# A recurrent attention step whose streamed weights are spread over the step and whose ring slots are released one by one

## The chip, the cores and the metric

The kernel runs on one core of one Trainium2 chip. The metric is device time in microseconds (us), the median over several executions. TensorE (PE) multiplies, and its weight loads (PEld) overlap its matmuls; ScalarE (ACT), VectorE (DVE) and GpSimd (POOL) do the rest, and SyncE (SP) does nothing here but issue DMA transfers.

## The reference

Two branches over 2048 rows of width 1024 are mixed by a gate. Branch A is a recurrence over 64 segments of 32 rows: each step attends over 8 memory rows and 32 new rows (40 columns) with 32 heads of 128, and the first 8 rows of its result are the next step's memory. Branch B is a feed-forward layer of width 3584.

```python
for s in range(n_seg):                      # 64
    h = concatenate([mem, x[:, s*32:(s+1)*32]], axis=1)      # 40 rows
    q, k, v = (einsum('btd,dhe->bhte', h, W) for W in (Wq, Wk, Wv))
    p = softmax(where(mask, q @ k.T * scale, -1e9))
    o = einsum('bhte,hed->btd', p @ v, Wo)
    mem = o[:, :8]; outs.append(o[:, 8:])
b = (gelu(x @ w_gate) * (x @ w_up)) @ w_down
return g * a + (1 - g) * b                  # g = sigmoid((x * gate_w).sum(-1))
```

## The kernel before

There are two blocks, one after the other: the recurrent chain (lines up to 693) and the feed-forward part (lines 695 to 999). Only the chain is touched. Within each block every engine has an instruction list in the order in which the Python code emits it; engines meet only at semaphores, which are written out by hand.

**Weights.** Wq, Wo and the K weights of heads 0 to 15 (`kres`) stay in SBUF. The K weights of heads 16 to 31 and all V weights are streamed anew in each step: a *slab* is the weights of four heads, 1 MB, and a step needs twelve, eight of V and four of K. They go into `ring`, which has three slots. `emit_slab` (L268) puts one transfer on SP's queue (L277), and it waits until the slab three before it has been used.

**A step.** The projections are cut into *blocks*: one matrix and one head, eight accumulating matmuls with their weight loads (L603), 40 columns of a PSUM bank. Blocks are grouped into *chunks*, which alternate between two PSUM banks, and ScalarE copies a finished chunk to `qkvT` (L623, L625 for K and Q, L630 for V). With four groups of eight heads the order of chunks is: K and Q of group 0 (six heads, then two), V of group 0; the same for group 1; K and Q of groups 2 and 3; V of group 2; V of group 3. That is twelve chunks. Attention work is hung between chunks by `add_hook`: scores (`emit_scores`, L392) with the softmax on VectorE and ScalarE (L403 to L422), the transposes of V (`emit_vtr`, L444), of the probabilities (`emit_pt`, L466), and the product with V (`emit_pv`, L492). Scores follow the group's last K/Q chunk at once, V's transposes follow the V chunk at once, the probabilities' transposes come two chunks after the scores. After the last chunk come what is left of attention, the transposes of the next rows of x (L512), and 256 matmuls with Wo (L663); ScalarE copies their result to `a_evac` and, as memory, to the next step's `hT` (L677), for which the next step's first chunk waits. The result of a step is transposed (`emit_atr`, L536) after the next step's first chunk.

**How slots come free.** Only the last block of a chunk raises a semaphore, and a slab is free when its chunk is done:

```python
E("pe", mk, waits=bw, inc=(S_QKV_DONE, 1) if last else None)
if streamed and h % 4 == 3:
    slab_free_target[slab_index(mat, h)] = C + 1
    emit_slab(slab_emit_count[0])
```

A V chunk uses two slabs, so both slots come free at its end.

Of the kernel before, what the change touches and what calls it, by code (L numbers as in the profile page):

```python
# [7 lines left out]
ACTF = mybir.ActivationFunctionType  # L8
# [79 lines left out]
def bass_gated_mix__memory_aug_recurrent_mem_tr__geglu_ffn__prompt_kernel(  # L88
# [47 lines left out]
    with ExitStack() as es_top:  # L136
        cnt = [0]

        def new_sem(name):
            cnt[0] += 1  # L140
            h = es_top.enter_context(nc.semaphore(f"{name}_{cnt[0]}"))
            return _Sem(h)
# [3 lines left out]
        with ExitStack() as es:  # L146
# [43 lines left out]
            S_SLOT = [new_sem(f"slot{i}") for i in range(RING)]  # L190
            S_QKV_DONE = new_sem("qkvdone")
            S_QKV_EVAC = new_sem("qkvevac")
            S_PINIT = new_sem("pinit")
            S_XTR_DONE = new_sem("xtrdone")
            S_HT = new_sem("htready")
# [34 lines left out]
            E("pool", lambda e: e.dma_start(stage[32:64, :], xf[0:SEG, :]), inc=(S_XLOAD, 16))  # L230
            E("pool", lambda e: e.dma_start(stage[64:64 + M, :], mem0[:, :]), inc=(S_XLOAD, 16))

            chunk_list = []
            if NG_ATT >= 2:
                for gq in range(NG_ATT - 2):
                    chunk_list += [("kqa", gq), ("kqb", gq), ("v", gq)]
                gA, gB = NG_ATT - 2, NG_ATT - 1
                chunk_list += [("kqa", gA), ("kqb", gA), ("kqa", gB), ("kqb", gB), ("v", gA), ("v", gB)]
            else:
                chunk_list += [("kqa", 0), ("kqb", 0), ("v", 0)]  # L240
            NCH = len(chunk_list)

            def chunk_blocks(kind, gq):
                hs = list(range(gq * 8, gq * 8 + 8))
                if kind == "kqa":
                    return [(m, h) for h in hs[0:6] for m in ("k", "q")]
                if kind == "kqb":
                    return [(m, h) for h in hs[6:8] for m in ("k", "q")]
                return [("v", h) for h in hs]
# [5 lines left out]
            for kind, gq in chunk_list:  # L255
                for mat, h in chunk_blocks(kind, gq):
# [111 lines left out]
            for s in range(NSEG):  # L368
# [8 lines left out]
                def emit_scores(gq):  # L377
                    gg = att_base + gq
                    b = gg % 2
                    slot = gq % 2  # L380
                    waits = [(S_QKV_EVAC, kqb_evac_target[gq])]
# [146 lines left out]
                def emit_atr(sp):  # L528
# [12 lines left out]
                    if sp >= 1:  # L541
# [3 lines left out]
                    E("pool", lambda e, sp=sp: e.dma_start(a_scr[sp * SEG:(sp + 1) * SEG, :], stage[0:SEG, :]),  # L545
                      waits=[(S_ASTG, sp + 1)], inc=(S_ASTORE, 16))

                if s == 0:
                    xtr_last_evac_box = [xtr_last_evac]
                pos = {ck: i for i, ck in enumerate(chunk_list)}  # L550
                hooks = {}
                END = NCH

                def add_hook(k, fn):
                    k = min(k, END)
                    hooks.setdefault(k, []).append(fn)

                kqb_evac_target = {}
                v_evac_target = {}
                hook_pri = {}  # L560
                for gq in range(NG_ATT):
                    k_sc = pos[("kqb", gq)] + 1
                    k_vt = pos[("v", gq)] + 1
                    k_pt = k_sc + 2
                    k_pv = max(k_pt, k_vt) + 1
                    for k, pri, fn in ((k_sc, 1, lambda gq=gq: emit_scores(gq)), (k_vt, 0, lambda gq=gq: emit_vtr(gq)),
                                       (k_pt, 3, lambda gq=gq: emit_pt(gq)), (k_pv, 2, lambda gq=gq: emit_pv(gq))):
                        add_hook(k, fn)
                        hook_pri[fn] = (min(k, END), k, pri, gq)
                if s >= 1:  # L570
                    fn_atr = lambda: emit_atr(s - 1)
                    add_hook(1, fn_atr)
                    hook_pri[fn_atr] = (1, 1, -1, 0)

                for ci, (kind, gq) in enumerate(chunk_list):
                    C = chunk_base + ci
                    bank = C % 2
                    blocks = chunk_blocks(kind, gq)
# [8 lines left out]
                    for bi, (mat, h) in enumerate(blocks):  # L587
                        bw = list(cw) if bi == 0 else []
                        if s == 0:
                            if mat == "q":  # L590
                                bw.append((S_WQ[h // 4], 16))
                            if mat == "k" and h < KRES_H:
                                bw.append((S_KRES[h // 4], 16))
                        streamed = is_streamed(mat, h)
                        if streamed and h % 4 == 0:
                            i = slab_index(mat, h)
                            bw.append((S_SLOT[i % RING], 16 * (i // RING + 1)))
                        lhs_list = [lhsT_for(mat, h, kc) for kc in range(KC)]

                        def mk(e, lhs_list=lhs_list, bank=bank, bi=bi, cur=cur):  # L600
# [11 lines left out]
                    view = PB[bank][:, 0:len(blocks) * L]  # L612
                    aw = [(S_QKV_DONE, C + 1)]
                    gg = att_base + gq
                    if kind == "kqa" and gg - 2 >= 0:
                        aw.append((S_SC_DONE, gg - 2 + 1))
                    if kind == "v" and gg - 2 >= 0:
                        aw.append((S_VTR_DONE, gg - 2 + 1))
                    if kind in ("kqa", "kqb"):
                        nh = 6 if kind == "kqa" else 2  # L620
                        h0 = 0 if kind == "kqa" else 6
                        v3 = view.rearrange("p (hh m c) -> p m hh c", m=2, c=L)
                        E("act", lambda e, v3=v3, slot=slot, h0=h0, nh=nh: e.activation(  # L623
                            qkvT[:, slot, h0:h0 + nh, :], v3[:, 0, :, :], ACTF.Copy), waits=aw)
                        E("act", lambda e, v3=v3, slot=slot, h0=h0, nh=nh: e.activation(  # L625
                            qkvT[:, slot, 8 + h0:8 + h0 + nh, :], v3[:, 1, :, :], ACTF.Copy), inc=(S_QKV_EVAC, 1))
                        if kind == "kqb":
                            kqb_evac_target[gq] = C + 1
                    else:
                        E("act", lambda e, view=view, slot=slot: e.activation(  # L630
                            qkvT[:, slot, 16:24, :], view.rearrange("p (hh c) -> p hh c", c=L), ACTF.Copy),
                          waits=aw, inc=(S_QKV_EVAC, 1))
                        v_evac_target[gq] = C + 1
                    assert S_QKV_EVAC.n == C + 1
                    for fn in hooks.get(ci + 1, []) if (ci + 1) < END else []:
                        fn()
# [396 lines left out]
```

## Time and profile before

| | |
|---|---|
| median of 5 runs | 4465.7 us (4456.75 to 4469.58) |
| profiled execution, its own time | 4458.04 us |
| span of the profiled execution | 4456.3 us |
| TensorE matmul busy, share of the span | 73% |
| TensorE weight loads busy | 65% |
| VectorE, ScalarE, GpSimd busy | 25%, 21%, 2% |
| mean granted TensorE clock | 0.748 |
| DMA, mean over the span | 221 GB/s |

The span runs from the first to the last instruction. Engines overlap, so shares do not add up. The granted clock is a share of 2.4 GHz; 0.50 is the lower level, 1.2 GHz. "issue" is a wait for nothing that the profile shows. Matmuls are pipelined and the end of one is modelled, so starts are the better measure of pace.

### The profile page before, as it was taken

What the parts mean: (1) busy time and instruction counts of PE and PEld (TensorE: products, weight loads), DVE (VectorE), ACT (ScalarE), POOL (GpSimd) and SP (SyncE); (2) the same over time, 40 slices, a digit from 0 to 9 for tenths busy, and PEclk for the clock granted to TensorE, in tenths of its full rate; (3) what the DMA queues carried; (4) which work ended last, traced back from release to release, by engine and by line L of the source; (5) the groups of instructions that cost most, each with busy time, mean ns of one, the idle gap of its engine ahead of it and who ended that gap; (6) DMA issues with size and microseconds to landing.
All of it is one profiled execution on the core that took longest, in us unless ns stands there. A gap on an engine that the chain in (4) does not pass through costs nothing. (4 is left out here: it accounts for less than half of the span.)

```text
span 4456.3 us, 169380 instructions
## 1 busy us (share of the span) xinstructions
PE 3266.0 (73%) x79440; PEld 2899.5 (65%) x79512; DVE 1122.7 (25%) x2577; ACT 947.2 (21%) x2818; POOL 82.0 (2%) x165
## 2 busy tenths in 40 slices
PE   3677777777777677777767677677777766699998
PEld 3666666666666666666666666666666666577776
DVE  1222222212222222222212222222222212355555
ACT  1122221222222222212212222222222111122222
POOL 0000000000000000000000000000000000000000
PEclk7777676767667777776767676777777766799999
DMA  9677676767777676766767777676767666766665
GB/s 327 209 223 226 216 224 213 226 218 222 226 230 231 215 220 208 224 213 213 230 212 231 230 231 230 212 221 213 226 211 233 215 213 200 233 209 204 214 207 166
DMA packets 945191, 982.96 MB, mean 221 GB/s; under 512 B 17256, under 2 KB 930664, under 8 KB 944496
## 3 DMA queue, kind: packets, MB, share of 16 engines
q1 hardware_dynamic: 937904, 955.31, 67.8%
q0 software_dynamic: 6592, 16.81, 1.2%
q8 instruction: 628, 10.29, 1.0%
q14 instruction: 67, 0.55, 0.0%
HBM read 963.66 MB, written 8.39 MB: 218 GB/s over the span
## 5 line engine op out<-in xcount | busy, mean ns | idle before, releaser
L603 PE MATMUL pb<-hT,ring 128*128 128x40 bf16 x24576 | 992.7, 194 | 680.9 <-DMA ring<-in_A_Wv_dram 385.9
L603 PEld LDWEIGHTS pb<-hT,ring 128*128 128x128 bf16 x24576 | 848.8, 106 | 760.6 <-DMA ring<-in_A_Wv_dram 314.6
L603 PE MATMUL pb<-hT,wq 128*128 128x40 bf16 x16384 | 798.6, 189 | 56.7 <-issue 53.6
L603 PEld LDWEIGHTS pb<-hT,wq 128*128 128x128 bf16 x16384 | 618.9, 102 | 51.5 <-issue 48.4
L663 PE MATMUL pb<-oT,wo 128*128 128x40 bf16 x16384 | 513.3, 193 | 90.4 <-issue 76.6
L663 PEld LDWEIGHTS pb<-oT,wo 128*128 128x128 bf16 x16384 | 500.2, 105 | 103.1 <-issue 82.7
L623 ACT ACTIVATE qkvT<-pb 128x240 bf16<-128x240 f32 (+1 forms) x512 | 155.4, 304 | 1180.8 <-PE pb L603 1180.8
L403 DVE SCALAR_TENSOR_TENSOR sm<-pb,mask 40x320 f32<-40x320 f32 x256 | 123.5, 482 | 1115.1 <-PE pb L392 1115.1
L603 PE MATMUL pb<-hT,kres 128*128 128x40 bf16 x8192 | 372.4, 181 | 19.6 <-ACT hT L677 18.2
L451 DVE COPY vsb<-pb 40x1024 bf16<-40x1024 bf16 x256 | 174.1, 680 | 763.7 <-PE pb L444 763.5
L444 PE MATMUL pb<-ident,qkvT 128*40 128x128 bf16 x2048 | 230.6, 280 | 144.7 <-ACT qkvT L630 134.3
L603 PEld LDWEIGHTS pb<-hT,kres 128*128 128x128 bf16 x8192 | 280.9, 96 | 42.3 <-ACT hT L677 25.2
L444 PEld LDWEIGHTS pb<-ident,qkvT 128*40 128x40 bf16 x2048 | 171.1, 130 | 174.9 <-ACT qkvT L630 164.3
L543 DVE COPY stage<-pb 32x1024 bf16<-32x1024 bf16 x64 | 43.4, 679 | 911.8 <-PE pb L536 911.8
L630 ACT ACTIVATE qkvT<-pb 128x320 bf16<-128x320 f32 x256 | 111.9, 437 | 737.6 <-PE pb L603 737.3
L892 PE MATMUL psh<-xTall,ringb 128*128 128x256 bf16 x1792 | 233.3, 273 | 0.6 <-DVE gall L855 0.6
L902 PE MATMUL psh<-xTall,ringb 128*128 128x256 bf16 x1792 | 233.1, 273 | 0.0
L954 PE MATMUL psB<-wd,GT 128*128 128x512 bf16 x824 | 213.3, 380 | 21.7 <-DVE GT L935 18.3
L414 ACT ACTIVATE sm<-sm,nmx 40x320 f32<-40x320 f32 x256 | 143.8, 562 | 387.5 <-DVE nmx L410 387.5
L892 PEld LDWEIGHTS psh<-xTall,ringb 128*128 128x128 bf16 x1792 | 175.5, 98 | 65.8 <-issue 0.6
L902 PEld LDWEIGHTS psh<-xTall,ringb 128*128 128x128 bf16 x1792 | 175.5, 98 | 21.0
L392 PE MATMUL pb<-qkvT 128*40 128x40 bf16 x2048 | 107.5, 191 | 77.2 <-ACT qkvT L625 42.2
(64 smaller groups left out, 2200.4 us busy)
## 6 DMA issues: line engine op xcount, KB each, us to landing
ring<-in_A_Wv_dram SPq DMA_DIRECT2D x512, 1024.0 KB, 6.8
ring<-in_A_Wk_dram SPq DMA_DIRECT2D x256, 1024.0 KB, 7.7
ringb<-in_B_w_gate_dram SPq DMA_DIRECT2D x56, 1024.0 KB, 5.3
ringb<-in_B_w_up_dram SPq DMA_DIRECT2D x56, 1024.0 KB, 7.9
wq<-in_A_Wq_dram SPq DMA_DIRECT2D x8, 1024.0 KB, 11.9
wo<-in_A_Wo_dram SPq DMA_DIRECT2D x8, 1024.0 KB, 13.9
wd<-in_B_w_down_dram SPq DMA_DIRECT2D x7, 1024.0 KB, 7.2
kres<-in_A_Wk_dram SPq DMA_DIRECT2D x4, 1024.0 KB, 12.3
```

The lines of the kernel that those rows point to most:

```text
L392: ins = e.matmul(PB[5 + b][0:L, i * L:(i + 1) * L], lhsT=qkvT[:, slot, 8 + i, :], rhs=qkvT[:, slot, i, :], start=True, stop=True)
L403: E("dve", lambda e, b=b: e.scalar_tensor_tensor(out=sm[:, b, :, :], in0=PB[5 + b][0:L, 0:8 * L].rearrange("p (h k) -> p h k", h=8), scala ...
L414: E("act", lambda e, b=b: e.activation(sm[:, b, :, :], sm[:, b, :, :], ACTF.Exp, bias=nmx[:, b:b + 1], scale=1.0), waits=[(S_NMX, S_NMX.n) ...
L444: ins = e.transpose(PBV[3][0:L, i * 128:(i + 1) * 128], qkvT[:, slot, 16 + i, :], ident[:, :])
L451: E("dve", lambda e, vb=gg % 2: e.tensor_copy(v_sb[:, vb, :, :], PBV[3][0:L, 0:8 * 128].rearrange("p (a d) -> p a d", a=8)), waits=dwaits, ...
L603: ins = e.matmul(PB[bank][:, bi * L:(bi + 1) * L], lhsT=lhs_list[kc], rhs=hT[:, cur, kc, :], start=(kc == 0), stop=(kc == KC - 1))
L623: E("act", lambda e, v3=v3, slot=slot, h0=h0, nh=nh: e.activation(qkvT[:, slot, h0:h0 + nh, :], v3[:, 0, :, :], ACTF.Copy), waits=aw)
L630: E("act", lambda e, view=view, slot=slot: e.activation(qkvT[:, slot, 16:24, :], view.rearrange("p (hh c) -> p hh c", c=L), ACTF.Copy), wa ...
L663: ins = e.matmul(dst_bank[:, fl * L:(fl + 1) * L], lhsT=wo_sb[:, kc, f * 128:(f + 1) * 128], rhs=oT_sb[:, kc, :], start=(kc == 0), stop=(k ...
L892: ins = e.matmul(ps_h[:, hb, 0:RG * 128], lhsT=ringb[:, i_g % RINGB, kc, col:col + 128], rhs=xT_all[:, kc, rows], start=(kc == 0), stop=(k ...
L902: ins = e.matmul(ps_h[:, hb, RG * 128:2 * RG * 128], lhsT=ringb[:, i_u % RINGB, kc, col:col + 128], rhs=xT_all[:, kc, rows], start=(kc == ...
L954: ins = e.matmul(ps_B[:, t * NHALF + hf, 0:WH], lhsT=GT[:, gb, t * 128:(t + 1) * 128], rhs=wd_sb[:, j, hf * WH:(hf + 1) * WH], start=(j == ...
```

## The change

The chunks are formed anew. Groups 0 to 2 are cut into halves of four heads, and a chunk holds K, Q and V of its four heads; the last group keeps K and Q of six heads, of two heads, and V of eight heads. There are nine chunks in place of twelve. Within a chunk `run_order` runs, for each four heads, all K blocks, then all Q blocks, then all V blocks, while the place in the PSUM bank stays by head. So the slabs are used in the order V0, V4, V8, V12, K16, V16, K20, V20, K24, K28, V24, V28 (the number is the first head of the four), and resident blocks lie between many of them.

A new semaphore, `S_SLABF`, is raised by the last block of a slab where that is not the chunk's last block, and the transfer that reuses the slot waits for it (or, as before, for the chunk).

Scores and V transposes of groups 0 and 1 are hung one chunk after the chunk that completes them, those of group 2 right after it, the probabilities' transposes one chunk after the scores (group 2: two chunks), and the product with V one chunk after both; what falls past the last chunk is sorted by a rank. A chunk is copied by one ScalarE instruction per matrix.

```diff
-            chunk_list = []
-            if NG_ATT >= 2:
-                for gq in range(NG_ATT - 2):
-                    chunk_list += [("kqa", gq), ("kqb", gq), ("v", gq)]
-                gA, gB = NG_ATT - 2, NG_ATT - 1
-                chunk_list += [("kqa", gA), ("kqb", gA), ("kqa", gB), ("kqb", gB), ("v", gA), ("v", gB)]
...
+            chunk_plan = []
+            for gq in range(NG_ATT - 1):
+                chunk_plan.append((list(range(8 * gq, 8 * gq + 4)), ("k", "q", "v")))
+                chunk_plan.append((list(range(8 * gq + 4, 8 * gq + 8)), ("k", "q", "v")))
+            gL = NG_ATT - 1
+            chunk_plan.append((list(range(8 * gL, 8 * gL + 6)), ("k", "q")))
+            chunk_plan.append((list(range(8 * gL + 6, 8 * gL + 8)), ("k", "q")))
+            chunk_plan.append((list(range(8 * gL, 8 * gL + 8)), ("v",)))
+            NCH = len(chunk_plan)
...
+            def run_order(ci):
+                heads, mats = chunk_plan[ci]
+                col = {b: i for i, b in enumerate(chunk_blocks(ci))}
+                return [(col[m, h], m, h) for q in sorted({h // 4 for h in heads})
+                        for m in mats for h in heads if h // 4 == q]
...
-                    waits.append((S_QKV_DONE, slab_free_target[i - RING]))
+                    waits.append(slab_free_target[i - RING])
...
-                    k_sc = pos[("kqb", gq)] + 1
-                    k_vt = pos[("v", gq)] + 1
-                    k_pt = k_sc + 2
+                    ckq, cv = c_kq_done[gq], c_v_done[gq]
+                    k_sc = ckq + 2 if ckq + 2 <= NCH - 1 else ckq + 1
+                    k_vt = cv + 2
+                    k_pt = k_sc + 1
                     k_pv = max(k_pt, k_vt) + 1
...
+                    if gq == NG_ATT - 2:
+                        k_sc, k_vt = ckq + 1, cv + 1
...
-                        last = (bi == len(blocks) - 1)
-                        E("pe", mk, waits=bw, inc=(S_QKV_DONE, 1) if last else None)
-                        if streamed and h % 4 == 3:
-                            slab_free_target[slab_index(mat, h)] = C + 1
+                        last = (ri == len(blocks) - 1)
+                        frees = streamed and h % 4 == 3
+                        E("pe", mk, waits=bw, inc=(S_QKV_DONE, 1) if last else ((S_SLABF, 1) if frees else None))
+                        if frees:
+                            slab_free_target[slab_index(mat, h)] = (S_QKV_DONE, C + 1) if last else (S_SLABF, S_SLABF.n)
                             emit_slab(slab_emit_count[0])
...
+                    for mi, m in enumerate(mats):
+                        lastc = (mi == nm - 1)
+                        E("act", lambda e, v3=v3, slot=slot, mi=mi, m=m, hh0=hh0, nh=nh: e.activation(
+                            qkvT[:, slot, midx[m] * 8 + hh0:midx[m] * 8 + hh0 + nh, :], v3[:, mi, :, :], ACTF.Copy),
+                          waits=aw if mi == 0 else [], inc=(S_QKV_EVAC, 1) if lastc else None)
```

## Rows read from the trace of the kernel before

**Rows 1.** Windows: stretch, length, busy us (instructions) by engine, clock, DMA share, GB/s.

```profile
2000.00:3000.00 1000.00, 716.05 (x20120) 658.47 (x20120) 214.31 (x505) 208.09 (x642) 16.87 (x34) 0.71 0.71 223
...
4100.00:4456.00 356.00, 333.23 (x2516) 248.74 (x2554) 185.41 (x405) 101.44 (x256) 8.37 (x14) 0.99 0.62 197
```

**Rows 2.** One source line, L677: durations, first and last start, forms.

```profile
L677 ACT ACTIVATE hT<-pb x126: 197/197/198, 113.3 to 3722.0; 128x32 bf16<-128x32 f32 x126
```

**Rows 3.** Time line of TensorE in one step: start, length, instruction [idle before, releaser].

```profile
2041.49 0.36 PE L603 MATMUL pb<-hT,kres 128*128 128x40 bf16 x8
...
2043.32 0.36 PE L603 MATMUL pb<-hT,wq 128*128 128x40 bf16 x8
...
2045.59 0.37 PE L392 MATMUL pb<-qkvT 128*40 128x40 bf16 x8 [0.46 <-ACT qkvT L625]
2045.90 1.79 PE L603 MATMUL pb<-hT,ring 128*128 128x40 bf16 x64
2048.22 0.62 PE L444 MATMUL pb<-ident,qkvT 128*40 128x128 bf16 x8 [0.53 <-ACT qkvT L630]
2048.77 0.37 PE L603 MATMUL pb<-hT,kres 128*128 128x40 bf16 x8
...
2056.50 1.99 PE L603 MATMUL pb<-hT,ring 128*128 128x40 bf16 x55 [2.75 <-issue]
2059.02 1.04 PE L444 MATMUL pb<-ident,qkvT 128*40 128x128 bf16 x8 [0.53 <-ACT qkvT L630]
2059.99 0.45 PE L603 MATMUL pb<-hT,ring 128*128 128x40 bf16 x8
...
2061.60 0.43 PE L603 MATMUL pb<-hT,ring 128*128 128x40 bf16 x8
...
2064.29 0.37 PE L603 MATMUL pb<-hT,ring 128*128 128x40 bf16 x8 [2.06 <-DMA ring<-in_A_Wk_dram]
...
2085.56 1.25 PE L603 MATMUL pb<-hT,ring 128*128 128x40 bf16 x32 [1.76 <-DMA ring<-in_A_Wv_dram]
...
2090.62 7.95 PE L663 MATMUL pb<-oT,wo 128*128 128x40 bf16 x256 [0.20 <-ACT oT L500]
2098.86 0.37 PE L603 MATMUL pb<-hT,kres 128*128 128x40 bf16 x8 [0.29 <-ACT hT L677]
```

**Rows 4.** TensorE's waits, 113 to 3722: waiter, releaser, total us, times, longest.

```profile
PE pb L603 <- DMA ring<-in_A_Wv_dram: 333.1, 206, 4.1
PE pb L603 <- DMA ring<-in_A_Wk_dram: 202.2, 153, 3.6
PE pb L603 <- issue: 135.0, 78, 2.9
PE pb L444 <- ACT qkvT L630: 130.0, 247, 0.5
PE pb L663 <- issue: 76.6, 58, 2.8
PE pb L392 <- ACT qkvT L625: 41.0, 144, 0.5
```

**Rows 5.** Windows within one step, columns as in rows 1.

```profile
2041.00:2045.00 4.00, 4.00 (x136) 3.86 (x136) 0.68 (x1) 0.71 (x3) 0.00 (x0) 0.95 0.02 4
...
2056.00:2060.00 4.00, 2.98 (x64) 2.66 (x63) 0.48 (x1) 0.44 (x1) 0.00 (x0) 0.50 0.10 29
...
2090.50:2092.00 1.50, 1.38 (x41) 1.38 (x42) 0.00 (x0) 0.34 (x2) 0.50 (x1) 0.50 1.10 366
```

**Rows 6.** The ring's transfers from 2000 to 2160.

```profile
DMA to landing us min/median/max: 5.4/7.2/9.9
```

**Rows 7.** Time line of VectorE: first and last operation of one softmax.

```profile
2046.01 0.48 DVE L403 SCALAR_TENSOR_TENSOR sm<-pb,mask 40x320 f32<-40x320 f32 x1 [1.06 <-PE pb L392]
...
2048.55 0.48 DVE L422 TENSOR_TENSOR pn<-sm,rrec 40x320 bf16<-40x320 f32 x1
```

**Rows 8.** DMA queues of the page: packets, MB, share of 16 engines.

```profile
q8 instruction: 628, 10.29, 1.0%
```

More of the change, by code (lines that the diff above doesn't have):

```diff
@@ L192, in bass_gated_mix__memory_aug_recurrent_mem_tr__geglu_ffn__prompt_kernel @@
             S_QKV_EVAC = new_sem("qkvevac")
+            S_SLABF = new_sem("slabfree")
             S_PINIT = new_sem("pinit")
@@ L231, in bass_gated_mix__memory_aug_recurrent_mem_tr__geglu_ffn__prompt_kernel, with chunk_blocks @@
             E("pool", lambda e: e.dma_start(stage[64:64 + M, :], mem0[:, :]), inc=(S_XLOAD, 16))
-            chunk_list = []
-            if NG_ATT >= 2:
-                for gq in range(NG_ATT - 2):
-                    chunk_list += [("kqa", gq), ("kqb", gq), ("v", gq)]
-                gA, gB = NG_ATT - 2, NG_ATT - 1
-                chunk_list += [("kqa", gA), ("kqb", gA), ("kqa", gB), ("kqb", gB), ("v", gA), ("v", gB)]
[L239 to L249, printed above, removed]
+            chunk_plan = []
[7 more added lines that the diff above has]
+            NCH = len(chunk_plan)
+            def chunk_blocks(ci):
+                heads, mats = chunk_plan[ci]
+                return [(m, h) for h in heads for m in mats]
+            def run_order(ci):
+                heads, mats = chunk_plan[ci]
+                col = {b: i for i, b in enumerate(chunk_blocks(ci))}
+                return [(col[m, h], m, h) for q in sorted({h // 4 for h in heads})
+                        for m in mats for h in heads if h // 4 == q]
+            c_kq_done = {}
+            c_v_done = {}
+            for gq in range(NG_ATT):
+                for ci in range(NCH):
+                    heads, mats = chunk_plan[ci]
+                    if any(h // 8 == gq for h in heads):
+                        if "q" in mats:
+                            c_kq_done[gq] = ci
+                        if "v" in mats:
+                            c_v_done[gq] = ci
             def is_streamed(mat, h):
@@ L254, in bass_gated_mix__memory_aug_recurrent_mem_tr__geglu_ffn__prompt_kernel @@
             slab_seq = []
-            for kind, gq in chunk_list:
-                for mat, h in chunk_blocks(kind, gq):
+            for ci in range(NCH):
+                for _, mat, h in run_order(ci):
                     if is_streamed(mat, h) and h % 4 == 0:
@@ L380, in emit_scores @@
                     slot = gq % 2
-                    waits = [(S_QKV_EVAC, kqb_evac_target[gq])]
+                    waits = [(S_QKV_EVAC, kq_evac_target[gq])]
                     if gg - 2 >= 0:
@@ L546, in emit_atr @@
                       waits=[(S_ASTG, sp + 1)], inc=(S_ASTORE, 16))
+                kq_first_seen = set()
+                v_first_seen = set()
                 if s == 0:
                     xtr_last_evac_box = [xtr_last_evac]
-                pos = {ck: i for i, ck in enumerate(chunk_list)}
                 hooks = {}
@@ L554, in add_hook @@
                 def add_hook(k, fn):
-                    k = min(k, END)
                     hooks.setdefault(k, []).append(fn)
-                kqb_evac_target = {}
+                kq_evac_target = {}
                 v_evac_target = {}
@@ L561, in bass_gated_mix__memory_aug_recurrent_mem_tr__geglu_ffn__prompt_kernel @@
                 for gq in range(NG_ATT):
-                    k_sc = pos[("kqb", gq)] + 1
-                    k_vt = pos[("v", gq)] + 1
-                    k_pt = k_sc + 2
+                    ckq, cv = c_kq_done[gq], c_v_done[gq]
+                    k_sc = ckq + 2 if ckq + 2 <= NCH - 1 else ckq + 1
+                    k_vt = cv + 2
+                    k_pt = k_sc + 1
                     k_pv = max(k_pt, k_vt) + 1
-                    for k, pri, fn in ((k_sc, 1, lambda gq=gq: emit_scores(gq)), (k_vt, 0, lambda gq=gq: emit_vtr(gq)),
-                                       (k_pt, 3, lambda gq=gq: emit_pt(gq)), (k_pv, 2, lambda gq=gq: emit_pv(gq))):
+                    if gq == NG_ATT - 2:
+                        k_sc, k_vt = ckq + 1, cv + 1
+                    lastg = (gq == NG_ATT - 1)
+                    for k, rank, fn in ((k_sc, 2, lambda gq=gq: emit_scores(gq)), (k_vt, 1, lambda gq=gq: emit_vtr(gq)),
+                                        (k_pt, 3, lambda gq=gq: emit_pt(gq)),
+                                        (k_pv, 4 if lastg else 0, lambda gq=gq: emit_pv(gq))):
                         add_hook(k, fn)
-                        hook_pri[fn] = (min(k, END), k, pri, gq)
+                        hook_pri[fn] = (rank, gq)
                 if s >= 1:
@@ L572, in bass_gated_mix__memory_aug_recurrent_mem_tr__geglu_ffn__prompt_kernel @@
                     add_hook(1, fn_atr)
-                    hook_pri[fn_atr] = (1, 1, -1, 0)
-                for ci, (kind, gq) in enumerate(chunk_list):
+                    hook_pri[fn_atr] = (-1, 0)
+                for ci in range(NCH):
                     C = chunk_base + ci
                     bank = C % 2
-                    blocks = chunk_blocks(kind, gq)
+                    heads, mats = chunk_plan[ci]
+                    blocks = chunk_blocks(ci)
+                    gq = heads[0] // 8
                     slot = gq % 2
@@ L586, in bass_gated_mix__memory_aug_recurrent_mem_tr__geglu_ffn__prompt_kernel @@
                         cw.append((S_QKV_EVAC, C - 2 + 1))
-                    for bi, (mat, h) in enumerate(blocks):
-                        bw = list(cw) if bi == 0 else []
+                    for ri, (bi, mat, h) in enumerate(run_order(ci)):
+                        bw = list(cw) if ri == 0 else []
                         if s == 0:
@@ L612, in bass_gated_mix__memory_aug_recurrent_mem_tr__geglu_ffn__prompt_kernel @@
                     view = PB[bank][:, 0:len(blocks) * L]
+                    nm = len(mats)
+                    v3 = view.rearrange("p (hh m c) -> p m hh c", m=nm, c=L)
                     aw = [(S_QKV_DONE, C + 1)]
                     gg = att_base + gq
[L615 to L632, printed above, removed]
@@ new lines, in bass_gated_mix__memory_aug_recurrent_mem_tr__geglu_ffn__prompt_kernel @@
+                    if gg - 2 >= 0:
+                        if ("k" in mats or "q" in mats) and gq not in kq_first_seen:
+                            aw.append((S_SC_DONE, gg - 2 + 1))
+                            kq_first_seen.add(gq)
+                        if "v" in mats and gq not in v_first_seen:
+                            aw.append((S_VTR_DONE, gg - 2 + 1))
+                            v_first_seen.add(gq)
+                    hh0 = heads[0] % 8
+                    nh = len(heads)
+                    midx = {"k": 0, "q": 1, "v": 2}
@@ new lines, in bass_gated_mix__memory_aug_recurrent_mem_tr__geglu_ffn__prompt_kernel @@
+                    for mi, m in enumerate(mats):
[3 more added lines that the diff above has]
+                          waits=aw if mi == 0 else [], inc=(S_QKV_EVAC, 1) if lastc else None)
+                    if ci == c_kq_done[gq]:
+                        kq_evac_target[gq] = C + 1
@@ L633, in bass_gated_mix__memory_aug_recurrent_mem_tr__geglu_ffn__prompt_kernel @@
+                    if ci == c_v_done[gq]:
                         v_evac_target[gq] = C + 1
                     assert S_QKV_EVAC.n == C + 1
-                    for fn in hooks.get(ci + 1, []) if (ci + 1) < END else []:
-                        fn()
+                    if ci + 1 < END:
+                        for fn in hooks.get(ci + 1, []):
+                            fn()
                 chunk_global[0] += NCH
```

## Prediction

> **What bounds the kernel now.** I read the per-stage windows first, then the step period, TensorE's list of waits, and one step on the time line. The windows [rows 1] show two regimes. In the recurrent part (a window of 1,000 us from 2000) TensorE is busy 716 us of 1,000 at a mean granted clock of 0.71 while the DMA engines are at 0.71 share and 223 GB/s; in the feed-forward part, from 4100, TensorE is 333 of 356 at 0.99. The diff touches only the recurrent part. Its period comes from the evictions of Wo's result into the next step's `hT` [rows 2]: 126 of them, two a step, from 113.3 to 3722.0; less the half of Wo between a step's two (some 4.0, from its 7.95 [rows 3]) that is 62 periods in 3604.7 us, 58.1 us each. Within these 62 steps TensorE waits [rows 4] 333.1 + 202.2 us for V and K slabs, 8.6 us a step; 130.0 + 41.0 us for ScalarE to copy Q, K, V out of PSUM, 2.75 us a step; and 135.0 + 76.6 us for "issue" at two lines, 3.4 us a step. The rest is work at the clock that was granted.
>
> Is it the DMA's rate that is short, or its timing? At best the engines moved 366 GB/s [rows 5], 1.0486 MB / 366 = 2.87 us a slab, so the twelve slabs of a step (eight V, four K) need 34.4 us of 58.1. In 2056 to 2060 the same engines moved 29 GB/s, and four us later TensorE stood 2.06 us for a slab [rows 3, 5]. So it is timing: three slots, all full during resident work, and two of them given back together at the end of a V chunk. From one resumption after a slab at 2064.29 to that at 2085.56 [rows 3] six more slabs came, 3.55 us each, not 2.87.
>
> **Prices.** A block (8 matmuls with loads) takes (2043.32 - 2041.49)/9 = 0.203 us near the clock's upper level, 2.4 GHz (0.95 granted from 2041 to 2045), and (2061.60 - 2059.99)/6 = 0.268 at 1.2 GHz (0.50 just before) [rows 3, 5]; four blocks 0.82 / 1.07. Scores are 0.31 (2045.59 to 2045.90) and, by the blocks' ratio, 0.38-0.41; I take 0.38, and the same pair for the probabilities' transposes and for PV. V's transposes are 0.55 (2048.22 to 2048.77) / 0.97 (2059.02 to 2059.99). Wo's 256 matmuls are 32 blocks: 6.5 / 8.6, the one shown 7.95. A slab issued alone lands after 5.4 us, the least seen [rows 6]; a second behind it takes 2.87 more.
>
> **The change, part by part.** No block, attention operation or byte is added: 96 blocks, 12 slabs, four attention groups a step stay. ScalarE's copies go from four triples of 6-head and 2-head K/Q and 8-head V (20 a step) to 18 + 5 = 23; ScalarE is busy 208 us of 1,000 [rows 1] and the copies lie under the next chunk's blocks, so I put them at nothing; uncovered, three more at the 130.0/247 = 0.53 us that one is waited for now [rows 4] would be 1.6 us a step. The new semaphore is raised by a matmul in place of none and waited on by SP, which does nothing else: nothing.
>
> *Slots go back singly.* Each slab is released by its own last block, so in the streaming stretch two transfers stay outstanding where pairs left one. *The stream is spread.* Resident K and Q blocks (8 per V slab in heads 0 to 15, 4 Q blocks per two slabs in 16 to 23) now lie between the slabs. I follow one step from the release r of V's first slab, fast / slow clock. Chunks 0 to 3 are TensorE's: their slabs leave at 0, 3.0/4.2 (the transposes of the former step's output included), 5.5/7.4 and 8.8/12.0, each reload lands 5.4 or more later and in time. Then K16 is released at 9.9/13.5; V16 lands at 11.3/12.8 (stall 0.6/0), released 12.1/15.6; pv0, scores 1 and transposes 1 take 1.16/1.73; K20 lands 14.2/17.4 (stall 0.9/0.1), released 15.0/18.5; V20 lands 17.1/20.3 (1.3/0.7), released 17.9/21.4; K24 20.0/23.2 (0.4/0); K28 22.9/26.1 (1.3/0.3); V24 25.8/29.0 (0.2/0); V28 28.7/31.9 (2.1/1.1), consumed at 29.5/33.0. Then the tail: pv2, transposes, probabilities, pv3, the x transposes, Wo, and the next chunk 0's twelve blocks, with the short waits the trace has there, 12.1/15.5. Period 41.6/48.5, the middle 45.0. Slab stalls left: 6.8/2.2 us instead of 8.6.
>
> *Scores and V transposes go one chunk later* than the copy they need for groups 0 and 1. That takes most of the 2.75 us: I count 1.2 left (group 2, whose hooks follow its chunk at once, behind a 0.3-us transpose; group 3, as now). This is in the sum above. What it costs: probabilities now follow scores by one chunk, not two. The softmax from 2046.01 to the end of the product at 2048.55 + 0.48 [rows 7] is 3.0 us; V's transposes and one chunk, 0.55 + 2.46 = 3.0, just cover it at the fast clock. At worst a few tenths for group 0; the others have stalls or more work between. If it did not cover at all, every transposes' wait would hold the next chunk's blocks in TensorE's queue and with them SP's next slab, up to 2 us for each of four.
>
> *What is not removed:* the issue waits, 3.4 us a step. I take them for late instruction loading: a queue "instruction" moved 628 packets, 10.29 MB [rows 8], at most 9.8 a step, and the waits stand inside runs of identical matmuls (2.75 us before 2056.50 [rows 3]). The section "Instruction fetch mechanics" of the Trainium skill's Runtime: NRT & Kernel Launch says that fetching is mostly hidden; by it nothing would be added to the 45.0. The trace disagrees with 3.4 us a step; the measurement decides.
>
> *Spacing.* Prices above use 2.87 us a slab. If the 3.55 of now stays, V28 lands at 5.4 + 8 x 3.55 = 33.8 after r, and the period is 33.8 + 0.82 + 12.1 = 46.7 fast or 33.8 + 1.07 + 15.5 = 50.4 slow, the middle 48.5. With the issue waits: 48.4 from the best spacing, 51.9 from the present one. Nothing tells which is nearer, since two outstanding is new but the instruction queue still cuts in; I take the middle, 50.1. That saves 8.0 us in each of 63 steps (the first is bound by the loading of resident weights): 504 us. The profiled execution took 4458.0 (span 4456.3); 4458 - 504 = 3954, and since it lies 7.7 us below the median of the runs shown, 3962: **3960**.
>
> **Rivals.** *The clock stays up* (chance 0.11). In rows of long unbroken work the clock is 0.99 to 1; in the stretch with stalls 2056 to 2060 it is 0.50 [rows 1, 5]. If shorter stalls keep it at 2.4 GHz, the period is 41.6 + 3.4 = 45.0 and the time 4466 - 63 x 13.1 = 3640. Against: even then 6.8 us of stalls and the issue waits remain. The section "Loop structure matters more than you think" of the Trainium skill's TensorE: Matmul & The Clock Gate says the same, that waits for transfers between matmuls let the clock drop and unbroken runs keep it; this trace agrees with those two rows.
>
> *The slab wait only moves* (0.15). Between the last slab's use and the next step's first release lie Wo and eight resident blocks, as before, and the ring fills there: at the slow clock V28 lands at 31.9, three more end at 40.5, and the next start is at 48.5 + 2.5 of latency (5.4 - 2.87), 10.5 us idle. Twelve slabs at 3.55 and that idle are 53.1; with Wo's issue waits (76.6/62 = 1.2), 54.3: 4466 - 63 x 3.8 = 4227.
>
> *Slower: instruction loading becomes the bound* (0.07). Place: TensorE's queue in the denser chunks 0 to 5, where slabs now flow while TensorE runs. Now 3.4 us over 9.8 packets is 0.35 us each; the longest wait was 2.9 [rows 4]. From 45.0, the period passes 58.1 when each costs 1.34. At 1.6 it is 60.7 and the time 4466 + 63 x 2.6 = 4630. For: transfers are outstanding nearly always. Against: 58 such waits in 62 steps at Wo, a dense run beside transfers, come to 1.2 us a step.
>
> *No change* (0.03): the stalls are all given back as issue waits or a lower clock; 58.1 as now, 4466.
>
> **How the numbers follow.** The forecast, periods from 46.7 (fast, present spacing) to 53.8 (slow, present spacing, issue waits whole), 3740 to 4195, has 0.64. The range 3690 to 4230 holds it, the second rival up to its price and the nearer half of the clock's case; it leaves out some 0.05 of the clock's case, 0.05 of the second, and the last two, 0.20 in all. A change of 0.2%, 9 us, is about what a measurement of this kernel can tell from none. Faster 0.90 (0.64 + 0.11 + 0.15), same 0.03, slower 0.07.
>
> **What would show it.** Period by the same evictions near 50; TensorE's waits for slabs from 8.6 to between 2 and 6 us a step; waits for ScalarE from 2.75 to some 1.2; DMA near 250 GB/s (12.58 MB in 50 us) without slices near 30 outside Wo and chunk 0; issue waits 3.4 or somewhat more; clock between 0.71 and 0.85; the feed-forward part unchanged. Wrong if issue waits grow by more than 5 us a step, if the clock sinks below 0.71, if the probabilities' transposes wait for VectorE, or if the slab waits fall by less than 3.

## The result and the profile after

The changed kernel takes 3964.8 us (median of 8 runs, 3960.7 to 3978.4) against 4466.8 (15 runs): a ratio of 0.888, 95% interval 0.887 to 0.889. The forecast was 3960. Its profiled execution has a span of 3964.0 us.

Two views of the changed kernel follow: the source line that copies Wo's result into `hT`, now L702, beside [rows 2], and the windows, beside [rows 1].

```profile
L702 ACT ACTIVATE hT<-pb x126: 197/198/199, 108.6 to 3235.2; 128x32 bf16<-128x32 f32 x126
```

```profile
2000.00:3000.00 1000.00, 789.14 (x23263) 736.13 (x23262) 244.06 (x580) 234.34 (x796) 19.85 (x40) 0.77 0.81 256
...
3600.00:3964.00 364.00, 340.86 (x2573) 254.86 (x2613) 189.04 (x413) 103.97 (x262) 8.37 (x14) 0.99 0.62 195
```

From the first of these copies to the last there are 3126.6 us where there were 3608.7: with the part of Wo between a step's two copies taken off as before, 62 steps of 50.3 us in place of 58.1. The stream went from 223 to 256 GB/s and the granted clock from 0.71 to 0.77; the feed-forward part is as it was. Of the 492 us by which the span shrank, 482 lie between these two evictions, 4.7 before the first (113.3 to 108.6) and 5.5 behind the last.

TensorE's waits over these steps, the answer to [rows 4]:

```profile
PE pb L624 <- issue: 237.5, 160, 3.5
PE pb L624 <- DMA ring<-in_A_Wv_dram: 107.7, 99, 3.3
PE pb L624 <- DMA ring<-in_A_Wk_dram: 102.8, 103, 2.8
PE pb L688 <- issue: 65.6, 49, 2.9
PE pb L506 <- ACT pT L487: 32.4, 62, 0.5
PE pb L406 <- ACT qkvT L651: 30.7, 86, 1.7
```

Slab waits fell from 535 to 211 us. The wait of V's transposes for ScalarE, 130.0 us before, is gone from the top of the list. "issue" is now the longest: 135.0 became 237.5 at the blocks.

One step on TensorE's time line (start, length, instruction, idle before):

```profile
2029.66 0.97 PE L624 MATMUL pb<-hT,ring 128*128 128x40 bf16 x32
...
2037.96 0.64 PE L624 MATMUL pb<-hT,ring 128*128 128x40 bf16 x19 [2.26 <-issue]
...
2042.41 0.98 PE L624 MATMUL pb<-hT,ring 128*128 128x40 bf16 x32
...
2044.36 0.98 PE L624 MATMUL pb<-hT,ring 128*128 128x40 bf16 x32 [0.15 <-DMA ring<-in_A_Wv_dram]
...
2049.26 1.23 PE L624 MATMUL pb<-hT,ring 128*128 128x40 bf16 x32 [2.21 <-DMA ring<-in_A_Wk_dram]
...
2052.17 1.25 PE L624 MATMUL pb<-hT,ring 128*128 128x40 bf16 x32 [0.62 <-DMA ring<-in_A_Wv_dram]
...
2055.45 1.25 PE L624 MATMUL pb<-hT,ring 128*128 128x40 bf16 x32
...
2058.11 0.57 PE L624 MATMUL pb<-hT,ring 128*128 128x40 bf16 x16 [0.38 <-DMA ring<-in_A_Wk_dram]
...
2062.04 1.25 PE L624 MATMUL pb<-hT,ring 128*128 128x40 bf16 x32
2064.07 1.25 PE L624 MATMUL pb<-hT,ring 128*128 128x40 bf16 x32 [0.78 <-DMA ring<-in_A_Wv_dram]
...
2068.76 4.28 PE L688 MATMUL pb<-oT,wo 128*128 128x40 bf16 x123 [0.20 <-ACT oT L514]
2074.40 4.40 PE L688 MATMUL pb<-oT,wo 128*128 128x40 bf16 x133 [1.36 <-issue]
2079.09 0.98 PE L624 MATMUL pb<-hT,kres 128*128 128x40 bf16 x32 [0.29 <-ACT hT L702]
```

V0 (2029.66) and K16 (2042.41) start without a slab wait; K20 waits 2.21 us, V20, K28 and V28 wait 0.38 to 0.78; Wo and one V slab are cut by an issue wait. From K20 to V28 five slabs take 14.81 us, 2.96 each, in this step.

### The profile page after: what moved, and what is told of

The parts are those of the page before. It is cut to its first block, busy times and chain, and to the rows that moved or that the text cites. A ratio compares the mean times of both kernels' runs of the same rounds, so it can differ in the third digit from the quotient of the medians.

```text
span 3964.0 us, 169254 instructions
## 1 busy us (share of the span) xinstructions
PE 3143.4 (79%) x79440; PEld 2821.9 (71%) x79512; DVE 1113.6 (28%) x2577; ACT 932.3 (24%) x3010; POOL 82.0 (2%) x165
## 5 line engine op out<-in xcount | busy, mean ns | idle before, releaser
L624 PE MATMUL pb<-hT,ring 128*128 128x40 bf16 x24576 | 855.2, 189 | 384.7 <-DMA ring<-in_A_Wv_dram 162.3
L624 PEld LDWEIGHTS pb<-hT,ring 128*128 128x128 bf16 x24576 | 767.5, 102 | 435.9 <-issue 220.7
L651 ACT ACTIVATE qkvT<-pb 128x160 bf16<-128x160 f32 (+3 forms) x1472 | 358.7, 309 | 1550.5 <-PE pb L624 1550.4
L624 PE MATMUL pb<-hT,wq 128*128 128x40 bf16 x16384 | 560.7, 187 | 113.0 <-issue 112.8
L624 PEld LDWEIGHTS pb<-hT,wq 128*128 128x128 bf16 x16384 | 504.5, 101 | 120.5 <-issue 120.4
L688 PE MATMUL pb<-oT,wo 128*128 128x40 bf16 x16384 | 512.3, 192 | 79.8 <-issue 65.6
L624 PE MATMUL pb<-hT,kres 128*128 128x40 bf16 x8192 | 259.8, 182 | 33.7 <-ACT hT L702 18.2
L624 PEld LDWEIGHTS pb<-hT,kres 128*128 128x128 bf16 x8192 | 232.4, 97 | 57.8 <-ACT hT L702 24.8
L458 PE MATMUL pb<-ident,qkvT 128*40 128x128 bf16 x2048 | 218.2, 270 | 20.9 <-issue 10.1
L917 PEld LDWEIGHTS psh<-xTall,ringb 128*128 128x128 bf16 x1792 | 175.7, 98 | 65.6 <-issue 0.6
L458 PEld LDWEIGHTS pb<-ident,qkvT 128*40 128x40 bf16 x2048 | 165.1, 126 | 31.3 <-ACT qkvT L651 18.3
L432 DVE TENSOR_REDUCE rsum<-sm 40x8 f32<-40x320 f32 x256 | 122.4, 478 | 160.8 <-ACT sm L428 160.8
L944 ACT ACTIVATE s<-psh 128x256 f32<-128x256 f32 x224 | 85.8, 383 | 289.4 <-PE psh L927 289.4
## 6 DMA issues: line engine op xcount, KB each, us to landing
wq<-in_A_Wq_dram SPq DMA_DIRECT2D x8, 1024.0 KB, 11.9
```

Source lines behind the costliest of these rows:

```text
L432: E("dve", lambda e, b=b: e.tensor_reduce(rsum[:, b, :], sm[:, b, :, :], AX.X, ALU.add), waits=[(S_EXP, S_EXP.n)], inc=(S_DVE_L, 1))
L458: ins = e.transpose(PBV[3][0:L, i * 128:(i + 1) * 128], qkvT[:, slot, 16 + i, :], ident[:, :])
L651: E("act", lambda e, v3=v3, slot=slot, mi=mi, m=m, hh0=hh0, nh=nh: e.activation(qkvT[:, slot, midx[m] * 8 + hh0:midx[m] * 8 + hh0 + nh, :] ...
L688: ins = e.matmul(dst_bank[:, fl * L:(fl + 1) * L], lhsT=wo_sb[:, kc, f * 128:(f + 1) * 128], rhs=oT_sb[:, kc, :], start=(kc == 0), stop=(k ...
L917: ins = e.matmul(ps_h[:, hb, 0:RG * 128], lhsT=ringb[:, i_g % RINGB, kc, col:col + 128], rhs=xT_all[:, kc, rows], start=(kc == 0), stop=(k ...
L944: E("act", lambda e, hg=hg: e.activation(s1[:, :], hg, ACTF.Square, scale=SQ_SCALE), waits=aw, inc=(S2_SQ, 1))
```

## The experiments

The ledger below has, per step, all of TensorE's waits between the first and the last of the 126 evictions, summed over all lines by what ended them; "rest" is the period less these three. "clock" is the mean granted clock of the same stretch. Ratios are to the kernel before, run on the same chip; a point below is one per cent of the time before.

| kernel | ratio (interval) | period | slabs | issue | ScalarE | rest | clock |
|---|---|---|---|---|---|---|---|
| before | 1 | 58.14 | 8.63 | 4.08 | 3.77 | 41.66 | 0.713 |
| after | 0.888 (0.887-0.889) | 50.34 | 3.39 | 5.59 | 1.61 | 39.75 | 0.769 |
| single release alone | 0.945 (0.943-0.948) | 54.07 | 5.54 | 3.85 | 3.83 | 40.85 | 0.749 |
| order alone | 0.954 (0.951-0.957) | 55.01 | 6.46 | 4.95 | 2.69 | 40.91 | 0.720 |
| after, chunk release | 0.932 (0.930-0.934) | 53.24 | 5.74 | 5.32 | 1.52 | 40.66 | 0.731 |
| after, hooks at once | 0.896 (0.894-0.898) | 50.73 | 4.22 | 3.99 | 2.79 | 39.73 | 0.771 |
| after, no stream | 0.703 (0.700-0.705) | 37.07 | 0 | 0.06 | 1.72 | 35.3 | 0.953 |
| before, no stream | 0.737 (0.734-0.739) | 39.43 | 0 | 0.02 | 4.09 | 35.3 | 0.962 |
| after, ring of four | 0.904 (0.903-0.906) | 51.41 | 0.52 | 9.19 | 1.64 | 40.06 | 0.756 |
| after, even K | 0.905 (0.903-0.908) | 51.44 | 3.34 | 6.51 | 1.70 | 39.9 | 0.770 |
| after, two outstanding | 0.895 (0.893-0.896) | 51.06 | 5.17 | 4.06 | 1.59 | 40.24 | 0.742 |
| ring of four, two outstanding | 0.900 (0.898-0.901) | 50.93 | 2.96 | 6.13 | 1.60 | 40.25 | 0.754 |
| after, half transfers | 0.920 (0.918-0.921) | 52.35 | 7.21 | 3.24 | 1.57 | 40.33 | 0.732 |

**Chunk release.** One part of the change undone.

```diff
-slab_free_target[...] = (S_QKV_DONE, C + 1) if last else (S_SLABF, S_SLABF.n)
+slab_free_target[...] = (S_QKV_DONE, C + 1)
```

> The changed kernel with one part undone: a slot is given back when its whole chunk is done, not at the slab's own last block. In chunks 0 to 3 nothing differs, the V slab ends its chunk. From K16 on, K16, K20 and K24 come free eight blocks (1.6 to 2.1 us) later, V24 four, K28 two. If single release carries the streaming stretch, slab waits rise from 3.4 to between 4.5 and 6.5 us a step and the time to 4030 to 4150 us. Rival, the order alone does it: 3953 to 3977, slab waits 3.4.

Measured 4152 us against 4454.5 of the kernel before beside it; slab waits 5.74. The rival falls. The DMA view of one step, in 40 slices (share in tenths, GB/s), shows how; first the changed kernel from 2028, then this one:

```profile
DMA  0005999936998999999999999999999999500000
GB/s 0 13 8 159 386 373 320 367 102 113 321 375 177 331 384 350 350 349 348 352 346 353 348 361 340 349 341 349 352 260 365 355 320 356 191 11 0 0 13 0
```

```profile
DMA  9979999379997799992289998000002799999928
GB/s 343 318 144 366 373 352 332 89 179 372 340 338 268 160 341 360 356 342 75 55 236 385 358 348 271 0 0 12 0 0 71 227 386 317 370 361 343 309 65 181
```

With single release the streaming stretch (from the slice of 331 on) runs near 350 GB/s, with one slice at 260; with chunk release it breaks down to 55 to 179 again and again. Of the change's 11.2 points, 4.4 go with this one expression.

**Single release alone**, put into the kernel before: the same expression, with the semaphore raised by the slab's last block.

> The kernel before with one part of the change: slots are given back at the slab's own last block, order and hooks as before. Of a V pair the first comes free four blocks (0.8 to 1.1 us) earlier, K slabs by up to eight blocks. My theory: a side effect of the order, slab waits fall from 8.6 by 0.5 to 2 us a step, time 4340 to 4435 us. Rival, single release is the main cause: slab waits near 4, time under 4200.

4206 us, slab waits 5.54 a step: neither. My theory, a side effect of the order, missed by 134 us; the rival's 4200 is missed by 6, and its "main cause" holds only in part, for the order alone is worth nearly as much. TensorE's waits of this run over its steps (waiter, releaser, total us, times, longest):

```profile
PE pb L604 <- DMA ring<-in_A_Wv_dram: 242.5, 180, 3.2
PE pb L604 <- issue: 186.0, 105, 3.6
PE pb L445 <- ACT qkvT L632: 130.1, 247, 0.5
PE pb L604 <- DMA ring<-in_A_Wk_dram: 101.2, 101, 2.9
```

K's slab waits halve (202.2 to 101.2) where V's fall by a quarter (333.1 to 242.5). The wait of V's transposes for ScalarE is untouched at 130.1 us; the next run shows what it hangs on.

**Order alone**: the new chunks (with their copies, one per matrix) with chunk release and the hooks at once.

```diff
-k_sc = ckq + 2 if ckq + 2 <= NCH - 1 else ckq + 1
-k_vt = cv + 2
-k_pt = k_sc + 1
+k_sc, k_vt = ckq + 1, cv + 1
+k_pt = k_sc + 2
...
-slab_free_target[...] = (S_QKV_DONE, C + 1) if last else (S_SLABF, S_SLABF.n)
+slab_free_target[...] = (S_QKV_DONE, C + 1)
```

> The new chunks and their order alone: release by chunk and hooks at once, as before the change. My theory: spreading the slabs among resident blocks is the largest part; the time is 4100 to 4250 us, slab waits 4.5 to 6.5 us a step, waits for ScalarE near 2.5. Rival, the order gives little without the two other parts: over 4350.

4242 us, in the forecast's band, but "the largest part" is wrong: 4.6 points, against 5.5 of single release alone. Nor is all of it the spread of the slabs. Of the 3.13 us that a step loses, slab waits give 2.17 and waits for ScalarE 1.08 (issue waits rise by 0.87, the rest falls by 0.75). Scores (L406) and V's transposes (L458) now wait so:

```profile
PE pb L406 <- ACT qkvT L650: 100.9, 193, 0.8
...
PE pb L458 <- ACT qkvT L650: 2.9, 19, 0.2
```

With the new chunks K, Q and V of a half group are copied together, and scores that come first take the one wait: 41.0 + 130.0 us of the kernel before are 100.9 + 2.9 here, with the hooks still at once. So the wait of V's transposes went with the chunks, not with the later hooks.

**Hooks at once**, in the changed kernel: the first five lines of the diff above.

> The changed kernel with one part undone: scores and V transposes follow the chunk that completes their group at once, probabilities' transposes two chunks after the scores. My theory: TensorE's waits for ScalarE come back from 0.6 to some 2.5 us a step, of which the slab waits hide a part, so 1 to 2 us a step and 4030 to 4090 us. Rival, the stream sets the pace and the waits for ScalarE only take the place of slab waits: 3950 to 3980 us.

3988.8 us, between the two and nearer the rival. Order and single release together, without the later hooks, give 10.4 points, about the sum of the two alone (10.1). The waits for ScalarE came back by 1.2 us a step, but only 0.4 of it as time (0.8 points by the ratios, some 0.55 us a step). TensorE's waits of this run:

```profile
PE pb L623 <- issue: 160.9, 116, 3.9
PE pb L623 <- DMA ring<-in_A_Wv_dram: 149.2, 118, 2.8
PE pb L623 <- DMA ring<-in_A_Wk_dram: 112.4, 114, 3.1
PE pb L406 <- ACT qkvT L650: 104.6, 205, 0.8
```

Scores wait 104.6 us for ScalarE (30.7 in the changed kernel), slabs 51 us more, and the issue waits at the blocks are 77 us shorter. In the ledger the issue waits give back 1.60 us a step, and the slab waits, which the expectation had as what hides the loss, rise by 0.83. That instructions go on arriving while TensorE stands for ScalarE would explain the first; it is not shown by itself.

**No stream**, from the changed kernel and from the one before: after step 0 nothing is loaded into the ring and nothing waited for, so the blocks use stale weights.

```diff
+if st >= 1:
+    slab_emit_count[0] = i + 1
+    return
...
-if streamed and h % 4 == 0:
+if streamed and h % 4 == 0 and s == 0:
```

> The changed kernel without the stream after the first step: the slabs of steps 1 to 63 are neither loaded nor waited for, their blocks read what lies in the ring, so the attention result is not the reference's. All TensorE instructions stay. If the issue waits come from slab traffic that delays instruction loading, they fall from 5 to under 1 us a step, the clock rises above 0.95 and the period is 35 to 38 us, the time 3000 to 3200 us. Rival, loading is too slow by itself for such a dense queue: issue waits of 4 us a step or more stay, the time is above 3300.

> The kernel before without the stream after the first step (slabs of steps 1 to 63 neither loaded nor waited for; the attention result is not the reference's). With no slab to wait for, only order and hooks differ from the changed kernel without the stream. My theory: it is slower than that one by the waits for ScalarE, 2.75 against 0.6, so by 1.5 to 2.2 us a step, 95 to 140 us. Rival, these waits are covered: within 20 us.

3133 us, as the theory had it. 3285 us is 152 more: the direction and the cause are the theory's, the size lies above its 95 to 140. The waits of the first:

```profile
PE pb L509 <- ACT pT L490: 32.4, 62, 0.5
PE pb L409 <- ACT qkvT L654: 28.1, 124, 0.5
PE pb L627 <- ACT hT L705: 17.9, 62, 0.3
PE pb L483 <- DVE pn L439: 15.1, 62, 0.2
...
PE pb L691 <- issue: 1.4, 3, 0.6
```

TensorE's instructions are the same, the pace is higher, and the issue waits are 0.06 us a step. So these waits come from the stream's traffic, not from how densely the instructions are used up. Here the later hooks and the order together are worth 2.4 us a step (39.43 to 37.07), as much as ScalarE's waits fall (4.09 to 1.72); under the stream the hooks bring back 1.2 us of such waits and 0.4 of time. And here the probabilities' transposes do wait for VectorE, 0.24 us, once a step, in the last group.

**Ring of four**: four slots, K of 12 heads resident, 13 slabs a step, one slab more in memory for the ring and one less for K.

```diff
-RING = 3
+RING = 4
...
-KRES_H = max(0, KRES_H - KRES_H % 4)
+KRES_H = min(12, max(0, KRES_H - KRES_H % 4))
```

> The changed kernel with a ring of four slots and K of 12 heads resident in place of 16 (the same memory): 13 slabs a step, and four are loaded ahead over Wo. If what is left is the stop of the stream while the ring is full, some 8 us a step, the fourth slot takes 2.9 of it and pays its own slab with it: 3930 to 3990, no gain. If slab waits come from latency with too few in flight, 3850 to 3930. Rival, more bytes in the same time delay instruction loading further: above 4000.

4033 us: the third case, as to the time. TensorE's issue and slab waits:

```profile
PE pb L624 <- issue: 379.4, 227, 3.7
PE pb L688 <- issue: 90.0, 60, 3.1
...
PE pb L624 <- DMA ring<-in_A_Wv_dram: 16.5, 27, 1.2
PE pb L624 <- DMA ring<-in_A_Wk_dram: 15.8, 27, 1.3
```

The slab waits are all but gone (0.52 us a step), and the issue waits have taken their place: 9.19.

**Even K**: K of heads 0-3, 8-11, 16-19 and 24-27 resident.

```diff
+RQ = [0, 2, 4, 6]
...
-return mat == "v" or (mat == "k" and h >= KRES_H)
+return mat == "v" or (mat == "k" and h // 4 not in RQ)
...
```

> The changed kernel with other resident K heads: 0-3, 8-11, 16-19, 24-27 in place of 0-15, the same memory and 12 slabs. Resident blocks then lie evenly through the step, so the stream runs from the first chunk on and less is left for the end. My theory: TensorE's pace sets chunks 0 to 3 now and the stream the rest; evened out, slab waits fall from 3.4 to some 2 us a step and the time by 60 to 130 us, to 3835 to 3905. Rival, the period is TensorE's work, its clock and instruction loading: slab waits fall but issue waits rise, 3940 to 3980.

4037 us, slower than both cases. Slab waits did not fall (3.34), issue waits rose to 6.51: not at the blocks (227.6 us against 237.5) but at Wo (91.9 against 65.6) and in attention (85 against 45). My theory, that the uneven spread of resident blocks costs slab waits, falls. The rival has the direction of the issue waits, not the slab waits.

**Two outstanding**, in the changed kernel and in the ring of four: a transfer also waits for the landing of the one two before it.

```diff
 waits.append(slab_free_target[i - RING])
+waits.append((S_SLOT[(i - 2) % RING], 16 * ((i - 2) // RING + 1)))
```

> The changed kernel with one more wait on SyncE's queue: a slab's transfer also waits until the slab two before it has landed, so at most two are outstanding (now three for about a fifth of the time). Theory: instruction loading waits behind the slabs outstanding; issue waits fall from 5.7 to between 4 and 5 us a step, slab waits rise by less than 0.5, time 3900 to 3955 us. Rival, any running transfer delays loading, however many stand behind it: issue waits 5.4 to 6, time 3955 to 3985.

> The kernel with four slots and 13 slabs a step, with the same limit of two outstanding transfers. Theory: its issue waits (above 9 us a step) come from three and four outstanding slabs, they fall to 4 to 6.5, and the time from 4033 to between 3900 and 3980 us. Rival, they come from the thirteenth slab and the denser work: issue waits stay above 8, time 4010 or more.

The issue waits went where the theories put them, 5.59 to 4.06 and 9.19 to 6.13. The times did not: 3990 and 4010 us, beyond the first rival's 3985 and at the second's 4010. In the first the slab waits rose by 1.78 and the clock fell to 0.742; in the second they rose by 2.44, so 4033 became 4010 and not 3900 to 3980.

**Half transfers**: each slab in two transfers of 512 KB, each with its own semaphore, at most three of these outstanding.

```diff
-E("sp", lambda e, ...: e.dma_start(ring[:, slot, :, :], slab_src(kind, hq)),
-  waits=waits, inc=(S_SLOT[slot], 16))
+for hf, sems in ((0, S_SLOT), (1, S_SLOTB)):
+    hw = list(waits) if hf == 0 else []
+    if i >= RING:
+        j, sj = (i - 2, S_SLOTB) if hf == 0 else (i - 1, S_SLOT)
+        hw.append((sj[j % RING], 16 * (j // RING + 1)))
+    E("sp", lambda e, ...: e.dma_start(
+        ring[:, slot, hf * 4:hf * 4 + 4, :], slab_src(kind, hq)[:, hf * 4:hf * 4 + 4, :]),
+      waits=hw, inc=(sems[slot], 16))
...
-bw.append((S_SLOT[i % RING], 16 * (i // RING + 1)))
+bw += [(x[i % RING], 16 * (i // RING + 1)) for x in (S_SLOT, S_SLOTB)]
```

> The changed kernel with each slab in two transfers of 512 KB (four of its eight row blocks each) and at most three of these outstanding, 1.5 MB. Theory: issue waits fall to 3 to 4.5 us a step while the rate stays, time 3860 to 3940 us. Rival, half as much in flight no longer covers a transfer's latency: slab waits rise by 1 to 3 us a step, which eats the gain, 3960 to 4080.

4098 us, a little above the rival. Both had a part: issue waits of 3.24, the lowest with a full stream, and slab waits of 7.21, 3.82 more where the rival had 1 to 3. That it is a transfer's latency which is no longer covered was not shown by itself.

## Why the prediction was right

*What bounds it.* The stream's timing was the limit, not its rate: with the same twelve slabs, TensorE waits 3.39 us a step for them in place of 8.63, inside the 2 to 6 of the forecast.

*Where the 7.80 us a step came from*, by the ledger: slab waits -5.24, waits for ScalarE -2.16, issue waits +1.51, the rest -1.91. For the rest no instruction was removed; the granted clock is 0.77 for 0.71, within the forecast's 0.71 to 0.85. Of ScalarE's 2.16 about half goes with the new chunks (3.77 to 2.69 with the order alone) and half with the later hooks (2.79 to 1.61). Without the stream, rest is 35.3 at clocks of 0.95 and 0.96. That the clock makes the whole rest is inferred from the order of these rows, not measured by itself.

*Slots singly and the spread.* The prediction followed both in one recurrence and did not divide them. The runs do: 5.5 and 4.6 points alone, 10.4 together. Of the recurrence's two columns the step shown comes near the slow one, but not by its blocks. V0 is released at some 2030.5 (its start and four blocks of 0.2); K20 starts 18.8 us later where the slow column lands it at 17.4, V28 33.6 us later where it lands at 31.9. Up to K16 nearly all blocks run at the fast price, and what brings the step to the slow column is one issue wait of 2.26, which the columns leave out; then K20's slab takes 6.9 us from issue to landing, not the 5.4 of one alone.

*The terms of the sum: luck.* The spacing was sized right. The sum took the middle between 2.87 and 3.55 us, 3.21; the step shown has 2.96, but over 60 steps the slabs from K20 to V28 land 3.23 us apart on average. Two other terms were off and nearly cancel. At its middle the 50.1 holds 6.2 us of slab waits (the mean of 6.8 and 2.2 at the best spacing and of 11.9 and 4.1 at the present one), 3.4 of issue waits and 40.5 of everything else; the ledger has 3.39, 5.59 and 41.4. The prediction added slab waits and issue waits as if neither could stand in for the other. In the runs the one goes up where the other goes down: their sum is 8.98 in the changed kernel and 9.09 to 9.85 in four of its variants (two outstanding, both with four slots, even K; 10.45 with half transfers), where the prediction's two make 9.6. So the sum of the two was near and its division was not. That slabs land while TensorE stands for instructions is the likely reason; it was not measured by itself. The prediction's third rival, loading that gets dearer as the stream gets denser, was at work at 1.5 us a step, not at the 10 it needed to decide.

*Hooks.* Waits for ScalarE at the lines of scores and V transposes were put at 1.2; they are 0.6 (L406 with 30.7 us and L458 with 5.1 over the steps). The prediction gave this gain to the later hooks; as the order alone shows, about half of it goes with the new chunks. The cost named, probabilities that wait for VectorE, is not in the list; without the stream it is 0.24 us, and in the last group, not in group 0 where the prediction looked for it. The prediction counted the gain, 2.75 to 1.2, in full; with the later hooks alone taken away, 1.2 us of waits come back and cost 0.4 us a step.

*The rivals.* The clock did not stay up (0.77; without a stream 0.95). The row of 0.50 from 2056 to 2060, which the prediction set beside waits for transfers, holds an issue wait of 2.75 us; a stretch of the kernel before with slab waits, 2076 to 2080, has 0.50 too. The slab wait did not merely move, but the stop that this rival named is there in full: eight of 40 slices at 0 to 13 GB/s, some 10.1 us of the step shown, where it had 10.5. What it had wrong is 3.55 us for each of the twelve slabs; the period less that stop leaves 3.35. Instruction loading does become the largest single wait (5.59), and with four slots it takes all that the slabs gave up.

*What the issue waits are.* The prediction took them for late instruction loading. The trace's record of single packets bears it out: the wait of 2.26 us before 2037.96 ends 1.42 us after a packet of 16,384 bytes on the queue "instruction" (2035.40 to 2036.54), and over the 62 steps of the changed kernel 242 of the 245 issue waits end 1.2 to 1.7 us after such a packet does. Of all moments in these steps 9% lie so. In the kernel before it is 163 of 164.

*What that section of the skill says.* The Trainium skill's Runtime: NRT & Kernel Launch, section "Instruction fetch mechanics", has fetching mostly hidden. The run without a stream agrees (0.06 us a step); with the stream it does not hold here (5.59).

*What stays open.* No tried version beats the changed kernel: the sum of slab and issue waits is 8.98 in it, 9.23, 9.71 and 9.09 in the limited and the four-slot versions, 9.85 with even K, 10.45 with half transfers. Why even K raises the issue waits was not settled. Nor is it divided how much the issue waits of the limited versions fell because instructions came sooner, and how much because they could come while TensorE stood longer for slabs. At Wo, where TensorE waits for no slab, two outstanding took them from 65.6 to 49.7 us, and from 90.0 to 80.9 with four slots.

## What to carry to other kernels

Give a ring's slot back at the last use of its own tile, not at the end of the group it was used in, and put work that needs no stream between the tiles: here the two were worth about 5 points each and added up, though about a third of what the new order gave was a wait for ScalarE and not for slabs. How even the spread is did not decide: with K resident evenly the kernel was slower, 4037 us. Before counting a removed wait as time, look at what else arrives during it: without a stream 2.4 us of waits for ScalarE were worth 2.4 us a step, with one 1.2 us of them were worth some 0.4 to 0.55. And when a deeper ring makes the slab waits vanish, look at the issue waits before calling it a gain.

## What the hardware showed that was not expected

A load of instructions comes late behind the slabs that are outstanding on the DMA engines. Taken from the packet records, from the end of an issue wait to the start of the next packet on the queue "instruction" the changed kernel shows a median of 1.15 us with no slab outstanding at that end, 1.33 with one, 3.51 with two and 4.20 with three. The ring of four has 1.14, 1.14, 3.44 and 4.18, and 5.20 with four (seven cases); with two outstanding at most, two slabs give 3.48; with half transfers, three halves (1.5 MB) give 3.00 and two (1 MB) 1.36. The packet itself takes 1.12 us in the changed kernel, and 1.02 without a stream.

Per step, TensorE's issue waits are 0.06 us with no stream, 3.24 with at most 1.5 MB outstanding, 4.06 with 2 MB, 5.59 with up to 3 MB, and with 13 slabs a step 6.13 at 2 MB and 9.19 at up to 4 MB. The limit alone does not set them: the kernel before, with up to 3 MB, has 4.08. Fewer outstanding bytes cost slab waits in their place: 7.21, 5.17 and 3.39 us at 1.5, 2 and 3 MB.
